# Batch 0's tail transposes, value products and squares in another order, V and w_out loads issued behind casts

## The chip, the cores and the metric

The kernel runs on one core of a Trainium2 chip. Its time is the device time of one execution in microseconds (us); lower is better. A profiled execution gives a trace of every engine: PE is TensorE (PEld its weight load), DVE is VectorE, ACT is ScalarE, POOL is GpSimd, SP is SyncE, which here only issues transfers. A "q" behind an engine's name (ACTq, SPq, POOLq) means its instruction queue, as for a DMA issue.

## The reference

Attention with a decay that depends on the position, over 8 batches of 8 heads, 576 positions and 64 numbers per head, and behind it a gated feed-forward network (FFN) over all 4608 tokens:

```python
scores = scale * np.matmul(q, k.transpose(0, 1, 3, 2))
cum = np.cumsum(np.maximum(s, 0.0), axis=-1)
bias = -(cum[:, :, :, None] - cum[:, :, None, :])
scores = np.where(causal, -1000000000.0, scores + np.minimum(bias, 0.0))
attn = softmax(scores)                       # rows, with the max taken off
x = np.matmul(attn, v)                       # then heads side by side: 4608 x 512

rms = np.sqrt(np.mean(x * x, axis=-1, keepdims=True) + 1e-06)
xn = x / rms * rms_g
g = xn @ w_gate                              # 512 x 1536
silu = g * (1.0 / (1.0 + np.exp(-g)))
val = xn @ w_val                             # 512 x 1536
out = silu * val @ w_out                     # 1536 x 512
```

All inputs and the output are float32. The kernel takes scores only between neighbouring blocks of 128 positions (the decay makes the others vanish) and checks at the end that this was allowed; a general version stands behind a branch.

## The kernel before

**Tiling.** A batch has five blocks of positions, four of 128 and a tail of 64 ("the tail" below), and its heads come in two halves, g = 0 for heads 0 to 3 and g = 1 for heads 4 to 7. The FFN goes over nine chunks of 512 tokens. A chunk has 12 gate blocks and 12 value blocks, each of four 128x512 matmuls (lines 730 and 739), and then four output blocks of 12 matmuls (line 752). Between a gate and a value block ACT takes the tanh (`T`, line 733), and DVE makes `U` from it (line 742) and `Ht` from U and the value block (lines 735 and 747).

**PSUM.** The banks are shared by tags: `psF` (four banks, for the FFN and for some transposes and scores), `psS` (two banks for one pair of scores), `psAV` (one bank, value products of g = 0) and `psT` (one bank, transposes and value products of g = 1). A new tile of a tag waits until the readers of the bank's last tile are done.

**Attention of one batch.** `load_kq` and `load_kq_tail` bring k and q as float32, `cast` and `cast_x` turn them into bfloat16 (`kqn`), `t_step` and `tail_step` transpose them on PE into `kqT` (tail_step, line 211: eight transposes for the two tails into one bank, and two copies by DVE for batch 0, lines 222 and 226). `s_step` makes scores of a key block with two query blocks and the exponentials `E` on ACT (line 299; line 315 for batch 0). `av_step` (line 333) multiplies E by V; a column of ones in `v_sb` gives the row sums, DVE takes their reciprocal (line 354) and scales (line 356) into `x_sb`. Its `norm` is a square with a running sum, on ACT (line 363) or DVE (line 367). `alpha` (two POOL operations, lines 376 and 379) makes 1/rms from it, `x_scale` (DVE, line 386) applies 1/rms and the gain, and x is transposed into `xnT`, by PE (`xt_step`, line 406) or by a DMA on SP's queue (`xt_dma`, line 397). Of batch 1, block (1,3) goes through PE, blocks 0 to 2 by DMA.

**The prologue** (lines 845 to 986) is an order written out by hand: each engine gets its instructions in the order of the text and waits where data are missing. It loads batch 0, transposes it, takes its scores (`s_first(kb, g)`: key block and half), value products (`do_av((0, qb, g))`), squares, alphas and four scalings, and transposes x for the first chunk. `fold_v` (POOL, line 330) multiplies V of batch 0 by the decay before its product. The gain is turned into a column (`g_col`, line 955) and spread over all rows in a bank (`gq`, line 958), which the first scalings read. `warm` and `stir` are matmuls without use. Behind the first scaling, SP issues four loads of k and q of batch 1.

**The FFN with attention in between.** After each gate and value block, and after each four output matmuls, `step` (line 655) advances a slot counter (36 slots a chunk) and places one piece of attention. In order it emits what is pending (the second half of a score's exponentials and its mask), a scaling that is due, one entry of `act_side` (loads on ACT's queue), then at odd slots one of `v_side` (loads on POOL's queue), then one of `pool_side`, then PE's pieces (`place`), then one of `dve_side`. Each entry has a condition, mostly a least slot. In chunk 0 `v_side` stops at slot 24, and `pool_side` from slot 30 to 33.

For chunk 0 the entries stand in lines 995 to 1016. On `pool_side` at slot 4, 6 and 8 are casts of batch 1 (`piece1`; that of slot 8 is q of heads 4 to 7), on `v_side` at slot 7 V blocks 0 and 1 of batch 1, at slot 9 w_out in two halves, then three more V blocks. `loads(2, 1, later, 14)` puts the q load of batch 2 on `act_side` from slot 14, its tail three slots later, and notes that slot as `raw`. `casts(2)` (line 495) puts five casts of that q and `over(1)`, which only notes the slot and queues later loads and transposes, on `pool_side`, each in a slot of its own, from seven slots after `raw`. In chunk 0 a slot is some 1.1 to 1.2 us.

Of the kernel before, what the change touches and what calls it, by code (L numbers as in the profile page):

```python
# [26 lines left out]
def kernel(  # L27
# [12 lines left out]
    nc = tc.nc  # L40
# [6 lines left out]
    NSC = 5  # L47
# [6 lines left out]
    def rows(c):  # L54
        return 128 if c < 4 else 64
# [49 lines left out]
    def psF():  # L105
        return pp.tile([128, DM], FP32, name="psF", tag="F", bufs=4)
# [10 lines left out]
    def psAV16():  # L117
        return pp.tile([128, 8, 128], BF16, name="psAV16", tag="AV", bufs=1)

    def psT():  # L120
        return pp.tile([128, 8, 128], BF16, name="psT", tag="T", bufs=1)

    def psT32():
        return pp.tile([128, 512], FP32, name="psT32", tag="T", bufs=1)


    def load_kq(eng, b, w, h0=0, h1=H):
        src = k if w == 0 else q
        eng.dma_start(
            out=kq32[:, w, h0:h1, 0:256],  # L130
            in_=src[b, h0:h1, 0:512, :].rearrange("h (p r) d -> p h (r d)", r=4))

    def load_kq_tail(eng, b, w):
        src = k if w == 0 else q
        eng.dma_start(
            out=kq32[0:64, w, :, 256:320],
            in_=src[b, :, 512:576, :].rearrange("h p d -> p h d"))

    def cast(eng, b, w, r0, r1, h0=0, h1=H):
        o = kqn[:, b % 2, w, r0:r1, h0:h1, :]  # L140
        i = kq32[:, w].rearrange("p h (r d) -> p r h d", d=D)[:, r0:r1, h0:h1, :]
        if eng is nc.scalar:
            eng.activation(out=o, in_=i, func=AF.Copy)
        else:
            eng.tensor_copy(out=o, in_=i)

    def cast_x(eng, b, w, hp):

        if hp < HP:
            o = kqn[:, b % 2, w, 0:4].rearrange("p r h d -> p (r h d)")[:, hp * 512:hp * 512 + 512]  # L150
            o = o.rearrange("p (r h d) -> p h r d", r=4, h=2)
            i = kq32[:, w, 2 * hp:2 * hp + 2, 0:256].rearrange("p h (r d) -> p h r d", d=D)
            eng.tensor_copy(out=o, in_=i)
        else:
            cast(eng, b, w, 4, 5)

    def load_k(b, c):
        n = rows(c)
        nc.gpsimd.dma_start(
            out=kqn[0:n, b % 2, 0, c],  # L160
            in_=k[b, :, c * 128:c * 128 + n, :].rearrange("h p d -> p h d"))
# [19 lines left out]
    def load_v(b, c):  # L181
        n = rows(c)
        nc.gpsimd.dma_start(  # L183
            out=v_sb[0:n, b % 2, c, :, 0:64],
            in_=v[b, :, c * 128:c * 128 + n, :].rearrange("h p d -> p h d"))
# [22 lines left out]
            out=kqTn[:, b % 2, w, hp:hp + 2, 0:512].rearrange("d h (p r) -> d h p r", r=4),  # L208
            in_=pT.rearrange("d (h r) p -> d h p r", r=4))

    def tail_step(b):
        pT = psT()
        nw = 2 if b < XB else 1
        for w in range(nw):
            for hp in range(HP):
                i = w * HP + hp
                nc.tensor.matmul(
                    pT[:, i, :], lhsT=kqn[:, b % 2, w, 4, 2 * hp:2 * hp + 2, :],
                    rhs=ident_bf, is_transpose=True, start=(i == 0), stop=(i == nw * HP - 1))
        dst, src = kqTn[:, b % 2, 0, :, 512:576], pT[:, 0:HP, 0:64]  # L220
        if b == 0:
            nc.vector.tensor_copy(out=dst, in_=src)
        else:
            nc.scalar.activation(out=dst, in_=src, func=AF.Copy)
        if nw == 2:
            nc.vector.tensor_copy(out=kqTn[:, b % 2, 1, :, 512:576], in_=pT[:, HP:8, 0:64])
# [147 lines left out]
    def alpha(c0, c1, n=128):  # L374

        nc.gpsimd.tensor_scalar(  # L376
            out=al_all[0:n, c0:c1], in0=ss_all[0:n, c0:c1],
            scalar1=1.0 / DM, scalar2=EPS, op0=ALU.mult, op1=ALU.add)
        nc.gpsimd.tensor_tensor(  # L379
            out=al_all[0:n, c0:c1], in0=al_all[0:n, c0:c1],  # L380
            in1=mhalf[0:n, 0:c1 - c0], op=ALU.pow)
# [50 lines left out]
    done = {}  # L432
# [10 lines left out]
    pool_side, dve_side, v_side, act_side = [], [], [], []  # L443
    x_seq = []

    def at(*key):
        return done.get(key, 10 ** 6)

    def ready(lag, *key):
        return at(*key) + lag <= slot[0]  # L450
# [31 lines left out]
    def loads(b, w, when, lag):  # L482

        def main():
            load_kq(nc.scalar, b, w)
            last["L"] = slot[0]

        def tail():
            load_kq_tail(nc.scalar, b, w)
            done["raw", b, w] = last["L"] = slot[0]  # L490
        n = len(act_side)
        when(act_side, lag, [main, tail])
        act_side[n:] = [(lambda c=c: c() and slot[0] - last["L"] >= 3, f) for c, f in act_side[n:]]

    def casts(b):

        def key(c):
            load_k(b, c)  # L500
            done["K", b, c] = slot[0]
            if c == NSC - 1:
                check(b)

        def over(w):
            done["cast", b, w] = slot[0]
            if b + 1 < B and (w == 1 or b + 1 < KB):
                loads(b + 1, w, early, 4)
            if w == 1:
                x_seq.extend((b, ww, c) for c in range(NSC) for ww in ((1, 0) if b >= KB else (1,)))  # L510
            else:
                done["cast", b] = slot[0]
                check(b)

        def free(w):
            return ready(0, "check", b - 2, w) and (
                ready(0, "T", b - 2) if w == 0 and b < KB + 2 else
                b < XB + 2 or ready(4, "X", b - 2, w, 4))
        if b >= KB:
            pool_side.extend((lambda: free(0) and slot[0] % 2 == 0, lambda c=c: key(c)) for c in range(NSC))  # L520
        fns = [(1, lambda r=r: cast_x(nc.gpsimd, b, 1, r)) for r in range(NSC)]
        fns += [(1, lambda: over(1))]
        if b < KB:
            fns += [(0, lambda r=r: cast(nc.gpsimd, b, 0, r, r + 1)) for r in range(NSC)]
            fns += [(0, lambda: over(0))]
        pool_side.extend((lambda w=w: ready(7, "raw", b, w) and free(w), f) for w, f in fns)

    def after_tail(b):
        if b + 2 < B:
# [32 lines left out]
    def do_av(key, ps=None, act=False, apart=False):  # L562
        b, qb, g = key
        act = act or b > 1 or b == 1 and qb > 1
        norm = av_step(b, qb, g, ps, act)
        if g == 1 and not apart:
            norm()
        done["AV", b, qb, g] = slot[0]
        last["AV"] = slot[0]
        if b > 0 and g == 1:  # L570
            last["AVT"] = slot[0]
        if qb == 4 and g == 1:
            if b == 0:
                nc.vector.memset(v_sb[:, 0, :, :, 64:65], 1.0)
            after_av(b)
        return norm
# [190 lines left out]
    def load_wout(f0):  # L767
        nc.gpsimd.dma_start(
            out=wout_sb[:, f0:f0 + 6, :],
            in_=moe_w_out[f0 * 128:(f0 + 6) * 128, :].rearrange("(fc p) d -> p fc d", p=128))  # L770
# [74 lines left out]
    with tc.manual_schedule():  # L845
# [37 lines left out]
        def pairF():  # L883
            return (psF(), psF())

        def s_first(kb, g, pair=None):
            do_s((0, kb, g), pair)()
# [51 lines left out]
            fold_v(POOL, c)  # L939
        load_w(moe_w_gate, wg_sb, 3, 6)  # L940
        s_first(0, 1, pairF())
        s_first(1, 1)
        tail_step(0)
        done["T", 0] = 0
        s_first(2, 1, pairF())
        do_av((0, 0, 0))
        norms = [do_av((0, 0, 1), psT32(), act=True, apart=True)]
        s_first(3, 0)
        do_av((0, 1, 0))
        s_first(3, 1, pairF())  # L950
        norms += [do_av((0, 1, 1), psT32(), act=True, apart=True)]
        ps = psS()
        gq = ps[:, 0, :]
        nc.tensor.matmul(ps[:, 1, 0:CC], lhsT=g_in, rhs=ident_f[0:CC, 0:CC], is_transpose=True)
        nc.vector.tensor_copy(out=g_col, in_=ps[:, 1, 0:CC])
        do_av((0, 2, 0))
        for c in range(CC):
            nc.tensor.matmul(gq[:, c * 128:(c + 1) * 128],
                             lhsT=g_col[:, c:c + 1].to_broadcast([128, 128]), rhs=ident_f,
                             is_transpose=True, start=(c == 0), stop=(c == CC - 1))  # L960
        norms += [do_av((0, 2, 1), psT32(), act=True, apart=True)]
        do_av((0, 3, 0))
        norms += [do_av((0, 3, 1), psT32(), act=True, apart=True)]
        for norm in norms:
            norm(False)
        alpha(0, 2)
        alpha(2, 3)
        alpha(3, 4)
        warm(4)
        for qb in range(4):  # L970
# [24 lines left out]
        def put(queue, n, *fns):  # L995
            queue.extend((lambda: slot[0] >= n, f) for f in fns)
# [7 lines left out]
        put(v_side, 1, lambda: load_w(moe_w_gate, wg_sb, 6, 12))  # L1004
        put(v_side, 3, lambda: (load_w(moe_w_val, wv_sb, 6, 9), load_w(moe_w_val, wv_sb, 9, 12)))
        put(v_side, 5, lambda: (load_tail(0), load_tail(1)))
        put(v_side, 7, lambda: (load_v(1, 0), load_v(1, 1)))
        put(v_side, 9, lambda: (load_wout(0), load_wout(6)))
        later(v_side, 0, [
            lambda: load_v(1, 2), lambda: load_v(1, 3), lambda: load_v(1, 4)])  # L1010

        loads(2, 1, later, 14)
        loads(2, 0, later, 24)
        check(0, (0,))
        check(1)
# [193 lines left out]
```

## Time and profile before

| | us |
|---|---|
| median of 3 runs (lowest, highest) | 366.95 (366.31, 367.0) |
| the profiled execution's own time | 365.93 |
| its span, first to last instruction | 364.3 |
| first FFN matmul (chunk 0) | 27.68 |
| first matmul of chunk 1 on record | 69.40 |
| last output copy on ACT ends | 359.2 |

Busy time in some stretches of the span, in us:

| stretch | length | PE | DVE | ACT | POOL |
|---|---|---|---|---|---|
| 15.61 to 20.20 | 4.59 | 4.59 | 2.21 | 4.17 | 4.57 |
| 20.20 to 22.98 | 2.78 | 1.98 | 2.07 | 2.15 | 1.80 |
| 42.00 to 58.00 | 16.00 | 15.92 | 14.63 | 13.38 | 9.77 |
| 58.00 to 66.00 | 8.00 | 8.00 | 5.56 | 5.21 | 6.29 |
| 246.00 to 282.00 | 36.00 | 36.00 | 23.88 | 26.69 | 9.43 |

Loads of the stretch around the change, from issue to landing in us: V blocks of batch 1, in order, 8.1, 8.0, 16.0, 15.9 and 13.9; the two halves of w_out 8.7 and 14.3; q of batch 2 12.5 and its tail 9.7.

How to read the lines below: start and duration in us, engine, source line, operation, tile written from tile read, shapes, count, and in brackets how long the engine was idle before and what released it. Lines with a count are several instructions in one row. A matmul's duration includes its way through the array, so consecutive ones overlap; their spacing counts.

### The profile page before, as it was taken

The page shows a single profiled execution, that of the slowest core. Times are in us where ns is not written, and L with a number is a line of the kernel's source. Part 1 is how long each engine was busy: PE and PEld are TensorE (multiplying, and loading weights), DVE is VectorE, ACT ScalarE, POOL GpSimd, SP SyncE. Part 2 cuts the span into 40 slices and gives each one's busy share as a digit, 9 for nine tenths or more (in the row PEclk, how much of TensorE's full clock was granted, in tenths as well). Part 3 has the DMA queues.
Part 4 walks back from the last instruction along what each step waited for, and adds up shares of the span by engine and source line. Part 5 has one row for each costly group of instructions (what it writes and reads, how often), then busy time and mean ns, then how long its engine had stood idle before and what let it go on. Part 6 is the DMA issues. An engine that isn't in the chain of part 4 may idle for free. (4 is left out here: it accounts for less than half of the span.)

```text
span 364.3 us, 6978 instructions
## 1 busy us (share of the span) xinstructions
PE 350.6 (96%) x2383; PEld 161.5 (44%) x2383; DVE 274.2 (75%) x523; ACT 237.1 (65%) x612; POOL 176.3 (48%) x286
## 2 busy tenths in 40 slices
PE   5889999999999999999999999999999999999993
PEld 2445444443444444444444444444444444444441
DVE  6687988599887889689989889884588558827830
ACT  3978686467885788876787777777677644223321
POOL 6958848739556466879648823732222200000000
PEclk9999999999999999999999999999999999999999
DMA  7999999999959399949979944972300130020011
GB/s 224 130 189 291 186 239 204 185 219 192 187 139 108 69 191 141 168 120 163 167 198 173 144 109 106 108 95 59 101 14 17 43 108 3 0 88 29 1 47 73
DMA packets 126592, 45.81 MB, mean 126 GB/s; under 512 B 104980, under 2 KB 121880, under 8 KB 126552
## 3 DMA queue, kind: packets, MB, share of 16 engines
q0 software_dynamic: 62048, 11.93, 45.9%
q1 hardware_dynamic: 51872, 23.80, 31.1%
q10 hardware_dynamic: 12632, 9.59, 10.9%
q8 instruction: 19, 0.31, 0.4%
q14 instruction: 21, 0.17, 0.2%
HBM read 37.90 MB, written 9.44 MB: 130 GB/s over the span
## 5 line engine op out<-in xcount | busy, mean ns | idle before, releaser
L299 ACT ACTIVATE E<-psS,biasK 128x256 bf16<-128x256 f32 (+3 forms) x328 | 106.9, 413 | 19.5 <-PE psS L275 19.1
L730 PE MATMUL psF<-xnT,wg_sb 128*128 128x512 bf16 x432 | 111.1, 379 | 0.7 <-DVE U L742 0.4
L739 PE MATMUL psF<-xnT,wv_sb 128*128 128x512 bf16 x432 | 111.1, 379 | 0.0
L752 PE MATMUL psF<-wout_sb,Ht 128*128 128x512 bf16 x432 | 102.3, 379 | 0.0
L742 DVE SCALAR_TENSOR_TENSOR U<-T,psF 128x512 bf16<-128x512 f32 x108 | 73.6, 682 | 29.5 <-ACT T L733 29.5
L733 ACT ACTIVATE T<-psF 128x512 f32<-128x512 f32 x108 | 64.4, 597 | 43.6 <-PE psF L730 40.6
L308 POOL TENSOR_SCALAR_AFFINE_SELECT E<-E 128x512 bf16<-128x512 bf16 x64 | 45.3, 708 | 86.4 <-ACT E L299 86.0
L735 DVE TENSOR_TENSOR Ht<-U,psF 128x512 bf16<-128x512 bf16 x99 | 67.6, 683 | 7.1 <-PE psF L739 0.5
L730 PEld LDWEIGHTS <-wg_sb 128*128 128x128 bf16 x432 | 38.7, 98 | 45.6 <-issue 6.4
L752 PEld LDWEIGHTS <-Ht 128*128 128x128 bf16 x432 | 38.7, 98 | 42.1 <-issue 2.3
L739 PEld LDWEIGHTS <-wv_sb 128*128 128x128 bf16 x432 | 38.5, 98 | 42.4 <-issue 4.4
L757 ACT ACTIVATE osb<-psF 128x512 f32<-128x512 f32 x36 | 21.4, 595 | 34.4 <-PE psF L752 28.6
L386 DVE SCALAR_TENSOR_TENSOR xs_sb<-x_sb,al_all,g_row 128x512 bf16<-128x512 bf16 (+1 forms) x36 | 29.3, 813 | 12.7 <-POOL al_all L379 12.7
L183 POOL DMA_DIRECT2D v_sb<-in_v_dram x40 | 34.8, 872 | 0.3 <-issue 0.3
L363 ACT ACTIVATE xs_sb<-x_sb 128x512 bf16<-128x512 bf16 (+1 forms) x37 | 23.5, 636 | 16.4 <-DVE x_sb L356 16.3
L424 DVE TENSOR_TENSOR acc<-acc,mag 128x1280 bf16<-128x1280 bf16 x32 | 27.2, 862 | 0.2
L275 PE MATMUL psS<-kqT 64*128 64x256 bf16 (+2 forms) x304 | 25.9, 256 | 0.9 <-ACT kqT L200 0.5
L347 PEld LDWEIGHTS <-E 128*128 128x128 bf16 x320 | 21.7, 97 | 10.1 <-issue 0.2
L379 POOL TENSOR_TENSOR al_all<-al_all,mhalf 128x1 f32<-128x1 f32 (+2 forms) x39 | 22.9, 586 | 3.2
L341 PEld LDWEIGHTS <-E 128*128 128x128 bf16 x256 | 20.0, 98 | 7.8 <-DVE x_sb L356 0.6
L275 PEld LDWEIGHTS <-kqT 64*128 64x128 bf16 x320 | 9.4, 94 | 30.8 <-issue 29.5
L376 POOL TENSOR_SCALAR al_all<-ss_all 128x1 f32<-128x1 f32 (+2 forms) x39 | 9.6, 247 | 23.3 <-ACT xs_sb L363 20.1
(119 smaller groups left out, 300.3 us busy)
## 6 DMA issues: line engine op xcount, KB each, us to landing
out_dram<-osb SPq DMA_DIRECT2D x36, 256.0 KB, 2.2
kq<-in_q_dram ACTq DMA_DIRECT2D x6, 1024.0 KB, 7.2
v_sb<-in_v_dram POOLq DMA_DIRECT2D x32, 128.0 KB, 6.6
kq<-in_k_dram SPq DMA_DIRECT2D x4, 512.0 KB, 5.8
kq<-in_q_dram SPq DMA_DIRECT2D x4, 512.0 KB, 7.7
kq<-in_k_dram ACTq DMA_DIRECT2D x2, 1024.0 KB, 8.9
kqn<-in_k_dram POOLq DMA_DIRECT2D x16, 128.0 KB, 5.5
wout_sb<-in_moe_w_out_dram POOLq DMA_DIRECT2D x2, 768.0 KB, 11.5
```

The source lines that it names most:

```text
L183: nc.gpsimd.dma_start(out=v_sb[0:n, b % 2, c, :, 0:64], in_=v[b, :, c * 128:c * 128 + n, :].rearrange("h p d -> p h d"))
L275: nc.tensor.matmul(pair[par][:, j * W:j * W + M], lhsT=kT, rhs=qT, start=(j == 0 and not premask), stop=(j == nj - 1))
L299: nc.scalar.activation(out=eo, in_=ei, func=AF.Exp, scale=0.125, bias=biasK[:, kb, bh:bh + 1])
L308: nc.gpsimd.affine_select(out=Ev[:, :, 0:nq], in_=Ev[:, :, 0:nq], pattern=[[0, nh], [1, nq]], compare_op=ALU.is_ge, fill=0.0, base=0, chan ...
L386: nc.vector.scalar_tensor_tensor(out=xs_sb[0:n, (b * NSC + qb) % NX, :], in0=x_sb[0:n, (b * NSC + qb) % NX, :], scalar=al_all[0:n, col:col ...
L424: nc.vector.tensor_tensor(out=acc[:, sl], in0=acc[:, sl], in1=mag[:, sl], op=ALU.max)
L730: nc.tensor.matmul(Gp, lhsT=wg_sb[:, cc, fs], rhs=xnT[:, cc, x0:x0 + DM], start=(cc == 0), stop=(cc == CC - 1))
L733: nc.scalar.activation(out=T, in_=Gp, func=AF.Tanh, scale=0.5)
L735: nc.vector.tensor_tensor(out=Ht[:, fb - 1, :], in0=pend[0], in1=pend[1], op=ALU.mult)
L739: nc.tensor.matmul(Vp, lhsT=wv_sb[:, cc, fs], rhs=xnT[:, cc, x0:x0 + DM], start=(cc == 0), stop=(cc == CC - 1))
L742: nc.vector.scalar_tensor_tensor(out=U, in0=T, scalar=1.0, in1=Gp, op0=ALU.add, op1=ALU.mult)
L752: nc.tensor.matmul(Op, lhsT=Ht[:, fb, tb * 128:(tb + 1) * 128], rhs=wout_sb[:, fb, :], start=(fb == 0), stop=(fb == FB - 1))
```

## The change

In the prologue, the tail transposes of batch 0 go into the bank of `psAV` instead of `psT`, and stand before the scores of key block 1 for heads 4 to 7. The value products of block 1 both stand before the last scores, (3, 1). The squares (`norms`), which stood together behind all value products, are put one by one: the first ahead of the exponentials of (3, 1), the second behind them, the third and fourth each behind its own value products. The alphas are grouped 0, then 1 and 2, then 3, instead of 0 and 1, then 2, then 3. The g transposes stand between the two halves of block 3.

In chunk 0, V of batch 1 goes from slot 7 to 9, w_out from 9 to 11, so the three V blocks behind move by two slots too; q of batch 2 goes from slot 14 to 17. The five q casts of batch 2 begin five instead of seven slots after `raw`, and the last one and `over(1)` share a slot.

```diff
-    def tail_step(b):
-        pT = psT()
+    def tail_step(b, pT=None):
+        pT = psT() if pT is None else pT
@@
         fns = [(1, lambda r=r: cast_x(nc.gpsimd, b, 1, r)) for r in range(NSC)]
-        fns += [(1, lambda: over(1))]
+        if b == 2:
+            fns[-1] = (1, lambda: (cast_x(nc.gpsimd, b, 1, NSC - 1), over(1)))
+        else:
+            fns += [(1, lambda: over(1))]
...
-        pool_side.extend((lambda w=w: ready(7, "raw", b, w) and free(w), f) for w, f in fns)
+        pool_side.extend((lambda w=w: ready(5 if (b, w) == (2, 1) else 7, "raw", b, w) and free(w), f) for w, f in fns)
@@
         s_first(0, 1, pairF())
+        tail_step(0, psAV16())
+        done["T", 0] = 0
         s_first(1, 1)
-        tail_step(0)
-        done["T", 0] = 0
         s_first(2, 1, pairF())
         do_av((0, 0, 0))
         norms = [do_av((0, 0, 1), psT32(), act=True, apart=True)]
         s_first(3, 0)
         do_av((0, 1, 0))
+        norms += [do_av((0, 1, 1), psT32(), act=True, apart=True)]
+        norms[0](False)
+        alpha(0, 1)
         s_first(3, 1, pairF())
-        norms += [do_av((0, 1, 1), psT32(), act=True, apart=True)]
+        norms[1](False)
         ps = psS()
         gq = ps[:, 0, :]
         nc.tensor.matmul(ps[:, 1, 0:CC], lhsT=g_in, rhs=ident_f[0:CC, 0:CC], is_transpose=True)
+        do_av((0, 2, 0))
         nc.vector.tensor_copy(out=g_col, in_=ps[:, 1, 0:CC])
-        do_av((0, 2, 0))
+        norms += [do_av((0, 2, 1), psT32(), act=True, apart=True)]
+        norms[2](False)
+        alpha(1, 3)
+        do_av((0, 3, 0))
         for c in range(CC):
             nc.tensor.matmul(gq[:, c * 128:(c + 1) * 128],
                              lhsT=g_col[:, c:c + 1].to_broadcast([128, 128]), rhs=ident_f,
                              is_transpose=True, start=(c == 0), stop=(c == CC - 1))
-        norms += [do_av((0, 2, 1), psT32(), act=True, apart=True)]
-        do_av((0, 3, 0))
         norms += [do_av((0, 3, 1), psT32(), act=True, apart=True)]
-        for norm in norms:
-            norm(False)
-        alpha(0, 2)
-        alpha(2, 3)
+        norms[3](False)
         alpha(3, 4)
@@
-        put(v_side, 7, lambda: (load_v(1, 0), load_v(1, 1)))
-        put(v_side, 9, lambda: (load_wout(0), load_wout(6)))
+        put(v_side, 9, lambda: (load_v(1, 0), load_v(1, 1)))
+        put(v_side, 11, lambda: (load_wout(0), load_wout(6)))
...
-        loads(2, 1, later, 14)
+        loads(2, 1, later, 17)
```

## The prediction

> **What bounds the kernel.** I read the page's first part, then the busy time by stretch, then the timeline of the two places that the diff touches.
>
> ```profile
> PE 350.6 (96%) x2383; PEld 161.5 (44%) x2383; DVE 274.2 (75%) x523; ACT 237.1 (65%) x612; POOL 176.3 (48%) x286
> ```
>
> ```profile
> 22.98:27.68 4.70, 3.92 (x34) 1.75 (x31) 4.63 (x13) 3.61 (x9) 1.65 (x5) 1.00 1.15 229
> 27.68:42.00 14.32, 13.98 (x108) 7.25 (x108) 11.53 (x23) 10.05 (x23) 13.38 (x23) 1.00 1.32 249
> 174.00:210.00 36.00, 36.00 (x259) 16.20 (x258) 32.45 (x59) 27.87 (x79) 24.83 (x39) 1.00 1.55 168
> ```
>
> After the stretch and its length come busy time and count of PE, PEld, DVE, ACT and POOL, then the granted clock, the DMA share and GB/s. From 27.68, where the first chunk of the FFN begins, PE is full, at clock 1.00. So what moves the end is time without useful PE work: the prologue up to 27.68, and stalls later. A late step costs later chunks nothing more. Four 128x512 matmuls take 0.865 from start to start, four transposes 0.22; beyond such spacings, chunk 0 loses 0.87 at 38.65, 0.14 at 33.63 and 0.14 at 50.55.
>
> **The prologue** ends in a chain over ACT, DVE and POOL:
>
> ```profile
> 17.12 0.29 DVE L222 COPY kqT<-psT 128x256 bf16<-128x256 bf16 x1 [2.29 <-PE psT L217]
> 17.87 1.09 ACT L315 ACTIVATE E<-psF 128x512 bf16<-128x512 f32 x2 [0.21 <-PE psF L275]
> ...
> 22.71 0.63 ACT L363 ACTIVATE xs_sb<-x_sb 128x512 bf16<-128x512 bf16 x1 [0.63 <-DVE x_sb L356]
> 22.73 0.20 PE L341 MATMUL psT<-v_sb,E 128*128 128x65 bf16 x1 [0.49 <-DVE x_sb L356]
> ...
> 23.40 0.42 DVE L356 TENSOR_TENSOR x_sb<-psT,rZ 128x256 bf16<-128x256 f32 x1
> ...
> 23.74 0.74 DVE L386 SCALAR_TENSOR_TENSOR xs_sb<-x_sb,al_all,psS 128x512 bf16<-128x512 bf16 x1
> ```
>
> Two things are visible. The tail transposes stand on PE between the scores of key blocks 1 and 2, and ACT is idle 0.21 for it. The value products hand psAV and psT back and forth with DVE, and the last half, at 22.73, waits for DVE; behind it come the four scalings, the transposes and the first FFN matmul.
>
> Tail step: 8 transposes cost 0.46 (16.46 to 16.92). Moved behind scores (0,1), they run at 15.23 to 15.69, while PE waits for psS until 15.61 anyway: 0.08 lost there. psAV was free since the copy of the paired transposes at 13.37. The two tail copies (0.29 and 0.28) fall into DVE's 2.29 of idling; that cover gone, they would cost 0.5. Exponentials (1,1) then start at 16.65, (2,1) at 17.73 instead of 17.87, (3,0) at 18.81 instead of 18.95.
>
> Value products: from PE start to the reciprocal 0.45 (18.84 to 19.29), then 0.22 to the scaling, 0.42 for it, 0.06 to hand the bank back. Block 0 starts at 17.39, its halves are scaled by 18.92; block 1 runs at 18.58 and 18.97, now ahead of scores (3,1), which go to 19.22. The v_sb fold of block 1 ends on POOL at 18.50: hidden by 0.08. Block 2 starts at 20.17 and 20.42; its second scaling, now behind the g_col copy (0.15), ends at 21.88. Block 3 starts at 21.32; the four g transposes (0.48) stand between its halves, so the second starts at 22.05 and its scaling at 22.72, 0.68 before 23.40. Squares take 0.61 on ACT: the first at 19.6, hence exponentials (3,1) at 20.26 instead of 19.99, which nothing needs before 22.05. The third starts at 21.92 instead of 22.71; 1.81 later (as 21.36 to 23.17 shows for a pair of columns) its alpha is ready, 23.73, and the second scaling goes at 23.78 instead of 24.47. The POOL operations of alpha stay six, grouped otherwise. I take **-0.65**; bounds -0.1 (one more handover of 0.55 comes in) and -0.8 (the third square's gain). SP's four loads for batch 1 come 0.65 earlier too, behind the scaling.
>
> **The stall at 38.65:**
>
> ```profile
> 35.86 1.79 POOL L183 DMA_DIRECT2D v_sb<-in_v_dram  x2
> 37.64 1.98 POOL L145 CAST kqn<-kq 128x256 bf16<-128x256 f32 x4
> ...
> 38.98 0.10 PEld L192 LDWEIGHTS <-kqn 128*128 128x128 bf16 x1 [0.25 <-POOL kqn L145]
> 39.51 0.68 DVE L367 SCALAR_TENSOR_TENSOR xs_sb<-x_sb 64x512 bf16<-64x512 bf16 x1
> ...
> 40.18 0.73 DVE L198 COPY kqT<-psT 128x512 bf16<-128x512 bf16 x1
> 40.83 0.66 DVE L735 TENSOR_TENSOR Ht<-U,psF 128x512 bf16<-128x512 bf16 x1
> 42.12 1.03 PE L730 MATMUL psF<-xnT,wg_sb 128*128 128x512 bf16 x4
> ```
>
> PE's transposes wait for POOL's casts, which stand behind two V issues (1.79). With V at slot 9 the casts run 35.9 to 37.4, done 1.2 before 38.65; their data (q, heads 4-7) landed at 35.05. PE gains up to 0.87, but DVE does not: from 38.26 it works back to back, and its copy at 40.18 starts as the square ends. The bank of the seventh gate block (42.12) is freed by Ht at 40.83 + 0.66 + 0.06 = 41.55. PE, 0.87 earlier, would start it at 41.25; it gets 41.5. The eighth is met (wanted at 43.68, its U done at 42.80 + 0.68 + 0.06 = 43.54), the ninth about met (46.25 against 46.32). So 0.6 of 0.87 stays: **-0.6**, bounds 0 (DVE's later steps take the rest) and -1.0 (DVE catches up in its 0.81 idle at 49.0, and the two waits of 0.14 go).
>
> What is moved behind: V(1,0), V(1,1), then w_out, then three V loads, in the same order on POOL's queue. Landings were 43.96 and 44.75, needed at 46.72; w_out 48.3 and 54.7, needed at 56.63 and about 58.3; V(1,2) landed at 58.1, needed at 58.73. That queue works without a break, so landings follow the queue, not the issue. The q load of batch 2 (1024 KB) on ACT's queue starts three slots later and leaves it room. Cost 0, up to +0.6 if V(1,2) lands when it did, as PE asks 1.2 earlier.
>
> **The cast merged with `over`.** `raw` is three slots later and the lag two less, so the five q casts of batch 2 shift by one slot; `over` stays at slot 29. The first is now behind alpha(1,1), the last between alpha(1,2) and alpha(1,3):
>
> ```profile
> 60.44 0.60 POOL L153 CAST kqn<-kq 128x512 bf16<-128x512 f32 x1
> 60.51 1.08 DVE L386 SCALAR_TENSOR_TENSOR xs_sb<-x_sb,al_all,g_row 128x512 bf16<-128x512 bf16 x1 [0.41 <-POOL al_all L379]
> 64.69 0.75 DVE L386 SCALAR_TENSOR_TENSOR xs_sb<-x_sb,al_all,g_row 128x512 bf16<-128x512 bf16 x1 [0.69 <-POOL al_all L379]
> 64.84 0.65 POOL L376 TENSOR_SCALAR al_all<-ss_all 128x1 f32<-128x1 f32 x1 [0.18 <-ACT xs_sb L363]
> 66.97 0.40 PE L406 MATMUL psT<-ident_bf,xs_sb 128*128 128x128 bf16 x4
> ```
>
> A cast just ahead of a scaling makes it 1.08 instead of 0.75. The last cast would start at 64.65, so: scaling (1,2) to 65.77, alpha(1,3) 0.48 later than now, and the transposes at 66.97, ready with no slack, 0.49 late. Chunk 1 starts at 69.40 only because xnT of block (1,2) lands at 69.27, 0.23 behind PE. So 0.49 - 0.23 = **+0.26**; bounds 0 (alpha's 0.65 at 64.84 shows it already blocked until the scaling ended) and +0.5.
>
> The Trainium skill, "SBUF — State Buffer", section "Who interferes with whom", says of this pair that VectorE operations with two SBUF inputs and a GpSimd operation that reads SBUF hold a shared port in turn, and the later one blocks entirely. By it the scaling would wait for the whole cast (0.6, where the row shows 0.33 of lengthening), and the item would be +0.5 and the sum -0.75.
>
> **Sum:** -0.65 - 0.6 + 0.26 = -1.0. Against the profiled execution (365.93, its span 364.3 and 1.6 around it) that is 364.9; the shown runs have a median 1.0 higher, 366.95, so **365.95**.
>
> **Cases.** About 0.2%, 0.73, is what a measurement can tell from no change.
> - Likeliest, **0.46**: as summed. Its own range is 365.5 to 366.5.
> - More, **0.20**: DVE catches up (-1.0), the cast is free: -1.65, 365.3. For it: DVE's idle 0.81 at 49.0. Against: the bank at 41.55.
> - Handed over, **0.24**: DVE's chain or V(1,2) takes back the whole of the second gain, leaving -0.65 + 0.26: 366.55. This is also what remains if the change does its new order but the stall merely moves. For it: DVE is busy 14.63 of 16.00 from 42 to 58; against: the banks' room.
> - Slower, **0.10**: the q load lands late.
>
> ```profile
> 43.60 0.40 ACTq L129 DMA_DIRECT2D kq<-in_q_dram  x1
> 47.97 0.65 ACTq L135 DMA_DIRECT2D kq<-in_q_dram  x1
> ```
>
> It took 12.5 to land at 56.10. Issued at slot 17 (now 47.97, less 1.2) it lands at 59.25, and POOL wants it at 60.44 - 1.2 = 59.24. On POOL the masks, alpha(1,2) and alpha(1,3) stand behind the waiting cast, and chunk 1's start behind those: each us late is a us. It is slower than before from 13.5 of landing on; at 14.25, half way to the slowest load of that stretch (16.0), it is 1.75 late: 367.7. Against it: POOL's queue, relieved until then, will have less left.
>
> Faster: 0.38 + 0.20 + 0.02 = 0.60. Same: 0.08 + 0.22 + 0.02 = 0.32. Slower 0.08. The range 365.1 to 367.1 leaves out about 0.07 below and 0.09 above.
>
> **What would show it.** Right: tail copies at about 16 on DVE; the first FFN matmul at 27.0; transposes after the second value step of block 4 at normal 0.22; a PE wait on Ht of some 0.25 before the seventh gate block; casts of batch 2 with no wait on DMA; the transposes of block (1,3) some 0.5 late by their spacing. Wrong: the first matmul at 27.5 or later, a PE wait for V in chunk 0's output part, POOL idle for kq.

## The result and the profile after

| | before | after |
|---|---|---|
| median of 22 runs each (lowest, highest), us | 367.0 (365.81, 367.87) | 368.76 (366.3, 371.57) |
| profiled execution, its span, us | 365.93, 364.3 | 368.94, 367.4 |
| first FFN matmul, us | 27.68 | 26.90 |
| first matmul of chunk 1 on record, us | 69.40 | 72.42 |
| from there to the end of the span, us | 294.9 | 295.0 |

The changed kernel is slower: ratio 1.0048, 95% interval 1.0027 to 1.0069, some 1.8 us. The last row places the loss: behind chunk 1's start the two profiled executions are alike, and chunk 0, from its first FFN matmul to chunk 1's, takes 45.5 us instead of 41.7. In the changed kernel the lines behind the prologue are numbered three higher (line 730 is 733, 752 is 755).

The page's first part and PE's useful work are as before:

```profile
PE 351.7 (96%) x2383; PEld 161.7 (44%) x2383; DVE 273.9 (75%) x523; ACT 237.1 (65%) x612; POOL 176.8 (48%) x286
```

The prologue went as intended. These lines are from the timeline of after (start, duration, engine, line, operation):

```profile
15.73 0.29 DVE L222 COPY kqT<-psAV 128x256 bf16<-128x256 bf16 x1 [0.64 <-PE psAV L217]
...
22.62 0.42 DVE L356 TENSOR_TENSOR x_sb<-psT,rZ 128x256 bf16<-128x256 f32 x1
22.96 0.74 DVE L386 SCALAR_TENSOR_TENSOR xs_sb<-x_sb,al_all,psS 128x512 bf16<-128x512 bf16 x1
...
26.90 1.02 PE L733 MATMUL psF<-xnT,wg_sb 128*128 128x512 bf16 x4 [0.25 <-ACT xnT L413]
```

The tail copies stand at 15.73 instead of 17.12, the last scaling of a value product at 22.62 instead of 23.40, the first FFN matmul 0.78 earlier.

Then chunk 0 loses it, and more. ACT's, POOL's and PE's timelines of after, up to and behind the stall that the change was to remove:

```profile
30.11 1.34 ACT L143 ACTIVATE kqn<-kq 128x256 bf16<-128x256 f32 x4 [1.55 <-DMA kq<-in_k_dram]
...
38.78 1.57 POOL L145 CAST kqn<-kq 128x256 bf16<-128x256 f32 x4 [2.13 <-DMA kq<-in_q_dram]
39.38 1.26 PE L192 MATMUL psT<-ident_bf,kqn 128*128 128x128 bf16 x4
40.30 1.79 POOL L183 DMA_DIRECT2D v_sb<-in_v_dram  x2
...
42.96 1.73 POOL L771 DMA_DIRECT2D wout_sb<-in_moe_w_out_dram  x2
...
45.27 0.90 POOL L183 DMA_DIRECT2D v_sb<-in_v_dram  x1
```

The kernel before issues V ahead of these casts, as the prediction showed, and w_out right behind them:

```profile
39.57 1.64 POOL L768 DMA_DIRECT2D wout_sb<-in_moe_w_out_dram  x2
...
42.08 0.95 POOL L183 DMA_DIRECT2D v_sb<-in_v_dram  x1
```

q of heads 4 to 7 of batch 1, issued at 25.47 instead of 26.25, landed at 38.8 instead of 35.0. POOL idles 2.13 for it. Its casts end at 40.35 instead of 39.62, by then as far behind before as PE is, so PE's four transposes are stretched from 0.4 to 1.26 as before. V now stands behind the waiting casts, with w_out behind it: they are issued 4.4 and 3.4 later than before, V of block (1,2) 3.2 later.

The DMA view of before, from 40 to 46 us, shows the busy share of the DMA engines in 40 slices, then queue, packets, MB moved and the time of the packets:

```profile
DMA  9999999999999999999999999999999999999999
q0 software_dynamic: 3809, 1.06, 204.3%
```

The same view of after:

```profile
DMA  9999645455533597999999966999999977199411
q0 software_dynamic: 2918, 0.47, 115.2%
```

q0 carries what POOL issues. It moves 0.47 MB instead of 1.06, and the DMA engines are about half idle from 40.6 to 42.1 and nearly idle from 45.5 on: little is queued. The end of chunk 0 pays for it (PE's timeline of before, then of after):

```profile
58.77 0.20 PE L347 MATMUL psAV<-v_sb,E 128*128 128x65 bf16 x1
...
69.40 1.02 PE L730 MATMUL psF<-xnT,wg_sb 128*128 128x512 bf16 x4
```

```profile
60.28 0.19 PE L347 MATMUL psAV<-v_sb,E 128*128 128x65 bf16 x1 [0.77 <-DMA v_sb<-in_v_dram]
72.39 0.56 PEld L733 LDWEIGHTS <-wg_sb 128*128 128x128 bf16 x4 [1.71 <-DMA xnT<-xs_sb]
72.42 1.02 PE L733 MATMUL psF<-xnT,wg_sb 128*128 128x512 bf16 x4 [1.61 <-DVE mag L418]
```

V of block (1,2) lands at 60.3 instead of 58.1, and PE waits 0.77 for it. xnT of block (1,2) lands at 72.3, and chunk 1 starts after a wait of 1.61, where the row of before names none (0.23 by the spacing). The last two lines are the same wait; the row of PE names `mag` of DVE, which has nothing to do with the FFN, the row of PEld names the DMA that was late.

The losses of chunk 0 against before, by the spacings of PE: transposes at 30.68 +0.67 and at 33.61 +0.74, at 39.38 0 (0.87 in both), V +0.92, chunk 1's start +1.54, and 0.14 less, which before lost at 50.55. That is 3.73 of the 3.80. The first two follow the row of ACT above: k of heads 0 to 3, issued 0.77 earlier, landed at 30.1 instead of 28.8, and ACT waits 1.55 for it. Beyond the usual spacing PE loses 1.55 at these two places in after and 0.13 in before, but also 1.10 to 1.57 in e3, e7 and e12 below, which have the prologue of before: it is the spread of k's landing in the main.

### The profile page after: what moved, and what is told of

Read it like the earlier page. It is cut to its first block, busy times and chain, and to the rows that moved or that the text cites. A ratio compares the mean times of both kernels' runs of the same rounds, so it can differ in the third digit from the quotient of the medians.

```text
span 367.4 us, 6978 instructions
## 1 busy us (share of the span) xinstructions
PE 351.7 (96%) x2383; PEld 161.7 (44%) x2383; DVE 273.9 (75%) x523; ACT 237.1 (65%) x612; POOL 176.8 (48%) x286
## 5 line engine op out<-in xcount | busy, mean ns | idle before, releaser
L755 PEld LDWEIGHTS <-Ht 128*128 128x128 bf16 x432 | 38.7, 98 | 42.1 <-issue 2.3
L760 ACT ACTIVATE osb<-psF 128x512 f32<-128x512 f32 x36 | 21.4, 595 | 35.6 <-PE psF L755 29.7
L275 PEld LDWEIGHTS <-kqT 64*128 64x128 bf16 x320 | 9.3, 94 | 30.7 <-issue 29.5
## 6 DMA issues: line engine op xcount, KB each, us to landing
wout_sb<-in_moe_w_out_dram POOLq DMA_DIRECT2D x2, 768.0 KB, 10.2
```

The costliest lines, as they stand in the source:

```text
L275: nc.tensor.matmul(pair[par][:, j * W:j * W + M], lhsT=kT, rhs=qT, start=(j == 0 and not premask), stop=(j == nj - 1))
L755: nc.tensor.matmul(Op, lhsT=Ht[:, fb, tb * 128:(tb + 1) * 128], rhs=wout_sb[:, fb, :], start=(fb == 0), stop=(fb == FB - 1))
```

## The experiments

P is the prologue's order alone, V the two slot numbers of V and w_out, Q the later q load of batch 2 with its casts; the change is P, V and Q together. Each row of the table has the median, the ratio to before, run beside it on the same chip, with its 95% interval, and from the profiled execution: the landing of batch 1's q of heads 4 to 7, the landing of V of block (1,2), PE's wait for that V, and PE's wait at chunk 1's start. Waits are those in the brackets of PE's rows, 0 where there is none. A landing is the issue plus a duration given to a tenth, so it is good to 0.1.

| kernel | us | ratio | q | V(1,2) | V wait | chunk 1 wait |
|---|---|---|---|---|---|---|
| before | 367.0 | | 35.0 | 58.1 | 0 | 0 |
| after (P, V, Q) | 368.76 | 1.0048 (1.0027 to 1.0069) | 38.8 | 60.3 | 0.77 | 1.61 |
| e1: P | 366.71 | 0.998 (0.9961 to 0.9999) | 34.6 | 59.1 | 0.62 | 0.47 |
| e2: V | 370.41 | 1.009 (1.0067 to 1.0113) | 33.8 | 60.6 | 2.13 | 0 |
| e3: Q | 367.65 | 1.0004 (0.9984 to 1.0024) | 38.4 | 59.5 | 0 | 1.40 |
| e4: V, Q | 367.74 | 1.0016 (0.9993 to 1.0039) | 35.7 | 59.3 | 0.89 | 1.32 |
| e5: P, V | 367.34 | 1.0021 (0.9996 to 1.0046) | 36.4 | 60.6 | 1.74 | 0.81 |
| e6: P, Q | 366.82 | 0.9994 (0.997 to 1.0017) | 37.6 | 58.2 | 0 | 1.19 |
| e7: V, w_out in slot 9 | 368.23 | 1.0025 (0.9999 to 1.0051) | 38.9 | 61.5 | 1.74 | 0.67 |
| e8: P, V(1,2) earlier | 366.43 | 0.9981 (0.9968 to 0.9995) | 35.7 | 53.1 | 0 | 0.41 |
| e9: P, V, Q, V(1,2) earlier | 366.69 | 1.0009 (0.9984 to 1.0033) | 35.2 | 49.1 | 0 | 1.20 |
| e10: P, V(1,1) later | 366.73 | 0.998 (0.9959 to 1.0) | 40.0 | 54.4 | 0 | 0.41 |
| e12: before, q late | 366.99 | 1.0008 (0.9987 to 1.0029) | 38.3 | 59.9 | 0.17 | 0.15 |
| e13: P, V, Q, q late | 368.13 | 1.003 (1.0011 to 1.005) | 36.6 | 59.8 | 1.66 | 1.48 |
| e14: P, Q, q late | 367.02 | 0.9992 (0.9974 to 1.0009) | 38.0 | 59.1 | 0 | 1.83 |

One profile is one execution, and executions of one kernel spread over 2 to 5 us here; the profile shows by which way time is lost, the ratio how much on the whole. Most kernels ran ten or more times, e2 only four times. The landing of q moves between 33.8 and 40.0 with no order by P, V or Q.

Of the expectations below, those of e1, e6, e7 and e9 were met by the ratio, in the range of the theory named first. e2 lost far more than expected, e3, e4, e5, e12, e13 and e14 less; e8 and e10 gained less, and e11 went the other way.

### The three parts alone: e1, e2, e3

e1 takes the prologue of the change alone:

```diff
+        tail_step(0, psAV16())
         s_first(1, 1)
-        tail_step(0)
...
+        norms += [do_av((0, 1, 1), psT32(), act=True, apart=True)]
+        norms[0](False)
         s_first(3, 1, pairF())
-        norms += [do_av((0, 1, 1), psT32(), act=True, apart=True)]
```

> Only the prologue's new order; loads and casts at the slots of before. Theory 'late loads': the first FFN matmul moves from 27.7 to about 26.9 as in the changed kernel, but the batch 1 loads of k and q do not land earlier, so the casts wait for them and give back part: 0 to -0.8 us against before. No wait of chunk 1 for xnT beyond 0.3. Rival 'earlier loads collide': the four loads, issued 0.77 earlier into the weight loads, land several us later, stalls of 0.7 to 0.9 at the transposes of batch 1, and most of the loss of the whole change is here: +1 to +2 us.

e2 takes the slots of V and w_out alone:

```diff
-        put(v_side, 7, lambda: (load_v(1, 0), load_v(1, 1)))
-        put(v_side, 9, lambda: (load_wout(0), load_wout(6)))
+        put(v_side, 9, lambda: (load_v(1, 0), load_v(1, 1)))
+        put(v_side, 11, lambda: (load_wout(0), load_wout(6)))
```

> Only V of batch 1 at slot 9 and w_out at 11. Theory 'late loads': the casts of slot 8 run right behind those of slot 6 if q has landed (35.05 in before), so the stall of 0.87 goes, DVE takes some back, and V block 2 lands later than PE wants it: -0.6 to +0.4 us. Rival: nothing lands later, -0.6 us.

e3 takes q of batch 2 at slot 17 with its shifted and merged casts alone:

```diff
-        loads(2, 1, later, 14)
+        loads(2, 1, later, 17)
...
+        if b == 2:
+            fns[-1] = (1, lambda: (cast_x(nc.gpsimd, b, 1, NSC - 1), over(1)))
```

> Only q of batch 2 at slot 17 with its casts one slot later, the last merged with over. Theory 'late loads': the traffic of ACT's queue moves into the time of the xnT transposes by DMA, of which the last then takes 6 us instead of 3.8; chunk 1 starts 1.0 to 1.5 us later by its own wait: +1.0 to +1.5 us. Rival: 0 to +0.3 us (the merged cast alone).

P alone is 0.7 us faster (0.998), its first FFN matmul at 27.08. V alone is slower by 0.9%, more than the whole change. Its PE timeline shows both sides of the edit:

```profile
38.41 0.39 PE L192 MATMUL psT<-ident_bf,kqn 128*128 128x128 bf16 x4
...
41.36 1.02 PE L730 MATMUL psF<-xnT,wg_sb 128*128 128x512 bf16 x4 [0.19 <-DVE Ht L735]
...
60.71 0.21 PE L347 MATMUL psAV<-v_sb,E 128*128 128x65 bf16 x1 [2.13 <-DMA v_sb<-in_v_dram]
```

Where q lands in time (33.8), the stall of 0.87 is gone, the transposes take 0.39, and a short wait on Ht stands in its place. The price comes 19 us later: 2.13 of waiting for V. Here the DMA engines are full from 40 to 46 in nearly every slice, but q0 moved 0.87 MB, not 1.06; the thin part is 43 to 45, with 0.27 MB where before has 0.39.

Q alone shows no difference in the ratio, against the +1.0 to +1.5 expected. Its profile has no wait for V, and a wait of 1.40 at chunk 1: the last transpose of x by DMA took 5.2 instead of 3.8.

### The parts in pairs: e4, e5, e6

e4 joins the edits of e2 and e3, e5 those of e1 and e2, e6 those of e1 and e3:

```diff
 # e4, e5
-        put(v_side, 7, lambda: (load_v(1, 0), load_v(1, 1)))
+        put(v_side, 9, lambda: (load_v(1, 0), load_v(1, 1)))
 # e4, e6
-        loads(2, 1, later, 14)
+        loads(2, 1, later, 17)
 # e5, e6
+        tail_step(0, psAV16())
```

> All of the chunk 0 schedule (V, w_out, q, casts), prologue as before. Theory 'late loads': V block 2 awaited 0.5 to 0.8 us, chunk 1 late by 1.4: +1 to +2 us, about the loss of the whole change plus the prologue's gain of 0.8. Rival 'earlier loads collide': -0.6 to +0.2 us.

> Prologue and V, w_out behind the casts, q of batch 2 at slot 14 as before. Theory 'queue runs dry': V and w_out, issued behind casts that wait for q of batch 1, leave POOL's transfer queue short of work between 40 and 46 us, V block 2 lands 2 us or more later, and q of batch 2 ahead of it makes it worse: +2 to +3 us against before. Rival 'sum of parts' (prologue -0.7, V and w_out +3.0): +2.3. What tells them apart is in the trace: bytes of that queue from 40 to 46 below 0.9 MB (before 1.06) and the landing of V block 2 at 60 or later.

> The whole change without V and w_out behind the casts. Theory 'queue runs dry': the loss of the whole change (+1.8) goes: -0.9 to +0.3 us against before, 1.5 or more below the whole change. Rival 'the late q costs chunk 1': still +0.7 or more, by a wait for xnT at the start of chunk 1.

Adding V raises the ratio in all four pairs: by 0.90% to before, 0.41% to P, 0.12% to Q, 0.54% to P and Q; on the mean 0.49%, 1.8 us. Adding Q gives +0.04, +0.14, -0.74 (to V) and +0.27%, about nothing. Adding P gives -0.20, -0.69, -0.10 and +0.32%, on the mean -0.17%. Single differences carry an uncertainty of some 0.3%, and the large ones, 0.90, -0.74 and -0.69, all rest on the four executions of e2, so only the signs of V and the means are used; without the pair of e2, V's mean is 0.36%, 1.3 us. A PE wait for V(1,2) of 0.77 to 2.13 is in all four kernels with V, and in those without it is 0.62 once and 0 else; a wait of 1.2 to 1.6 at chunk 1 is in all four with Q, and 0 to 0.81 in those without.

### Why V(1,2) is late: e7, e8, e9, e10

e7 moves V behind the casts and leaves w_out in its slot, so only V's 1.8 us of issue go past the casts:

```diff
-        put(v_side, 7, lambda: (load_v(1, 0), load_v(1, 1)))
-        put(v_side, 9, lambda: (load_wout(0), load_wout(6)))
+        put(v_side, 9, lambda: (load_v(1, 0), load_v(1, 1), load_wout(0), load_wout(6)))
```

> Before with V blocks 0 and 1 in slot 9, together with w_out, which so keeps its slot; the last three V blocks go from 11, 13, 15 to the same slots. Only the order V behind casts differs. Theory 'queue runs dry': V lands about as before, w_out later by the 0.9 that the two V issues take behind the casts less the stall they leave, V block 2 some 0.5 to 1.5 later than before: +0.3 to +1.5 us, well under the 3.0 of the full two-slot shift. Rival 'V behind casts alone is the loss': +3 us.

e8 has the prologue of the change, V(1,0) and V(1,1) as before, and V(1,2) between the halves of w_out (in e8, e9 and e10 it leaves the list of V loads behind them):

```diff
-        put(v_side, 9, lambda: (load_wout(0), load_wout(6)))
+        put(v_side, 9, lambda: (load_wout(0), load_v(1, 2)))
+        put(v_side, 11, lambda: load_wout(6))
```

> The prologue's new order, and V block 2 of batch 1 issued between the two halves of w_out; all else as before. Theory: in every run PE waits for V block 2 at the first value product of the output part, or only just does not; landed by 55 it takes 0.6 to 0.8 out of the prologue version, unless the second half of w_out or V block 3 then comes late: -0.8 to -1.6 us against before. Rival: the bound is the sum of the traffic and another transfer is late in its place (V block 3, xnT): -0.3 to -0.8, as the prologue alone.

e9 does this in the whole change, with the halves at slots 11 and 13:

```diff
-        put(v_side, 11, lambda: (load_wout(0), load_wout(6)))
+        put(v_side, 11, lambda: (load_wout(0), load_v(1, 2)))
+        put(v_side, 13, lambda: load_wout(6))
```

> The whole change, but V block 2 of batch 1 is issued between the halves of w_out (slots 11 and 13). Theory 'queue runs dry': the wait for V block 2 (0.8 in the whole change's profile) goes, the wait for xnT at the start of chunk 1 (1.2 to 1.6 in all kernels with the late q) stays: +0.3 to +1.2 us against before, some 0.8 under the whole change. Rival: the second half of w_out is late in its place: as the whole change, +1.8.

e10 keeps V(1,0) ahead of the casts and puts V(1,1) behind them, with V(1,2) ahead of the second half of w_out:

```diff
-        put(v_side, 7, lambda: (load_v(1, 0), load_v(1, 1)))
-        put(v_side, 9, lambda: (load_wout(0), load_wout(6)))
+        put(v_side, 7, lambda: load_v(1, 0))
+        put(v_side, 9, lambda: (load_v(1, 1), load_wout(0), load_v(1, 2)))
+        put(v_side, 11, lambda: load_wout(6))
```

> The prologue, V block 0 alone ahead of the casts of slot 8, V block 1 and V block 2 around the first half of w_out at slot 9, the second half at 11. Theory: the casts start 0.9 earlier, so the stall at the transposes of heads 4 to 7 shrinks from 0.87 to 0.2 or less where q has landed in time, and only one issue is held up where it hasn't: -0.8 to -1.6 us against before. Rival: w_out behind two V issues runs late: -0.3 to +0.5.

In e7 q landed at 38.9, though its prologue is that of before; POOL waited 2.23, V was issued at 40.37, q0 moved 0.64 MB from 40 to 46, and V(1,2) came at 61.5. In e8 and e9 V(1,2) comes at 53.1 and 49.1 and PE waits for no V. e8's POOL and PE timelines:

```profile
40.36 0.89 POOL L183 DMA_DIRECT2D v_sb<-in_v_dram  x1
...
69.76 1.02 PE L730 MATMUL psF<-xnT,wg_sb 128*128 128x512 bf16 x4 [0.41 <-DVE rZ L354]
```

So the V wait can be taken away by the order within POOL's queue, and with it the loss is no longer seen: e9 stands at 1.0009 where the whole change was 1.0048. e9's median is below before's, but four of its twelve executions took over 368, so its ratio is not below 1. e8, at 0.9981, is level with P alone (0.998): the wait of 0.62 in P's profile is gone, and the ratio shows no gain from it. e10 gives what P gives too: a split of the two V blocks brings nothing more. In its profiled execution, the slowest of its twelve (368.63), q came at 40.0, the stall grew to some 1.7, and q0 moved only 0.49 MB from 40 to 46; yet PE waited for no V, since V(1,2) stood ahead of the second half of w_out.

Bytes of q0 by stretch, in MB, tell how a late start reaches V(1,2):

| | 40 to 46 | 46 to 54 | V(1,2) lands |
|---|---|---|---|
| before | 1.06 | 1.00 | 58.1 |
| e2 | 0.87 | 1.01 | 60.6 |
| e4 | 0.87 | 1.20 | 59.3 |
| after | 0.47 | 1.40 | 60.3 |

In e4 and after, where q of batch 2 on ACT's queue (q10) comes later, part of what is lost by 46 is made up (issued at 47.41 and 48.73; 42.84 in e2, which makes up nothing). And once V's own turn has come, it shares with that load. The DMA view of after from 56 to 58:

```profile
q10 hardware_dynamic: 491, 0.48, 88.0%
q0 software_dynamic: 490, 0.06, 47.3%
```

Packet for packet the two get the same, byte for byte V gets an eighth, since its packets are small. The Trainium skill, "DMA: Bandwidth & Descriptors", section "Queues, rings and completion order", says that a DMA engine goes round the queues that have work and changes at packet boundaries. The equal counts of these two rows agree, and so do 238 against 240 packets in before from 50 to 52.

### The start of chunk 1: e11

P and Q with the load of k of batch 2 six slots later, to keep it away from the transposes of x by DMA:

```diff
-        loads(2, 0, later, 24)
+        loads(2, 0, later, 30)
```

> Prologue and late q of batch 2, with k of batch 2 six slots later too (30 instead of 24). Theory: chunk 1 waits for the last xnT transfer because q's and k's traffic on ACT's queue runs beside it; with k later, that wait falls from 1.2 to 0.4 or less: 0.6 to 1.0 us under the same kernel with k at 24 (which was level with before). Rival: the wait comes from the scaling and its alpha behind the shifted casts on POOL, and stays at 1.2: no change.

It took 386.69, ratio 1.0516 (1.0493 to 1.054): PE has new waits from 80 us on, the longest 2.88; that k, issued at 62.35, came too late for batch 2 is the likely reason and was not traced. Chunk 1's wait stayed at 1.39, and k still ran beside the last transfer, from 62.4 to 69.2. The run does not separate the theories. What it shows on the side: the first transpose of x by DMA, ahead of k's load, took 5.5, where the other profiles have 8.2 to 9.5 with k beside it.

The queues during the last transfer show the same. Before, from 66 to 68 (q1 is SP's queue):

```profile
q1 hardware_dynamic: 791, 0.41, 116.2%
```

After, same stretch:

```profile
q1 hardware_dynamic: 341, 0.31, 52.4%
q0 software_dynamic: 480, 0.06, 46.5%
q10 hardware_dynamic: 480, 0.18, 39.9%
```

Before, SP's queue has the engines nearly for itself; in after, the tail of k of batch 2 (issued on ACT's queue at 61.56 instead of 60.05, landed in 10.2 instead of 5.7) and POOL's loads share them, and the transfer takes 6.1 instead of 3.8.

### A q of batch 1 made late: e12, e13, e14

The load of q of heads 4 to 7 goes behind the four scalings, some 2 us later, in before (e12), in the whole change (e13) and in P with Q (e14):

```diff
-                for g in (0, 1):
-                    for w in (0, 1):
-                        load_kq(nc.sync, 1, w, 4 * g, 4 * g + 4)
+                for g, w in ((0, 0), (0, 1), (1, 0)):
+                    load_kq(nc.sync, 1, w, 4 * g, 4 * g + 4)
...
+        load_kq(nc.sync, 1, 1, 4, 8)
```

> Before, with one load moved: q of batch 1, heads 4 to 7, is issued on SP's queue behind the first check of magnitudes, some 2 us later, so that it always lands late. V and w_out stand ahead of the casts that wait for it. Theory 'a late q holds V and w_out only where they stand behind the casts': the stall at the transposes of heads 4 to 7 grows by what the landing is later than 37.6, w_out is held too, as it is behind the casts also here, but V isn't: +1 to +2 us against before. Rival: a late q costs both orders the same.

> The whole change with the same load moved. Theory: V, w_out and all behind are held by the casts, POOL's queue carries under 0.6 MB from 40 to 46 us, V block 2 lands at 60.5 or later: +3 to +4.5 us against before, 1.5 or more over the kernel of before with the same load moved. Rival: as far above it as the whole change is above before (1.8), or less.

> The whole change without V and w_out behind the casts, with the same load moved. Theory: as before with the load moved, less the prologue's 0.7, plus the wait for xnT: +0.8 to +2 us against before, 1.5 or more under the whole change with the load moved. Rival: level with the whole change with the load moved.

In the order of before a q that lands at 38.3 costs nothing that the ratio shows (up to 1.1 us by its interval): V stands ahead of the waiting casts and w_out right behind them, they were issued at 36.69 and 40.41, and q0 moved 0.96 MB from 40 to 46. e14 says the same with P and Q. In the whole change the load landed at 36.6, earlier than in the profile of after itself, so e13 did not make the case worse than it was; it lies at 1.003, 1.1 us, where +3 to +4.5 was expected. The theory that a late q alone makes the loss falls by e2 (q at 33.8, V wait 2.13). It does add: in after the late q took the gain of the second part away and held V and w_out for 2.13 more.

## Why the prediction was wrong

Forecast were 365.95 and a range up to 367.1; the median is 368.76.

**The prologue, -0.65: right up to the first FFN matmul, and not all of it is kept.** That matmul came 0.78 earlier in the two profiles, and e1's ratio is worth 0.7 us (0.0 to 1.4 by its interval). Over all profiles it stands at 27.2 to 27.7 with the old prologue and at 26.4 to 27.3 with the new, 0.5 earlier on the mean. That SP's four loads "come 0.65 earlier too" was right for their issue (0.77), but not for their landing: k came at 29.7 on the mean with the old prologue and at 29.5 with the new. So ACT, which casts this k, waits longer, and behind the transposes that follow (33.99 in before) PE is ahead by 0.2 on the mean, not 0.5 (six executions with the old prologue, ten with the new). That k and q landed later in after than in before does not need the earlier issue: e3 and e7, with the old prologue, had q at 38.4 and 38.9, and e1, with the new, at 34.6.

**The stall at 38.65, -0.6 of 0.87: right where q lands in time, and not so in the profile of after.** e2, e4 and e5 lost the stall and showed the wait on Ht that was foretold (0.25; measured 0.18 to 0.19 as a wait, 0.35 by the spacing in e2). But the step took q as landed at 35.05, the value of one execution, in which there were 2.6 us to the casts at 37.64. Moving V behind the casts spends that cover, and the landing spreads over 6 us. In after POOL waited, and PE's stall was 0.87 as before.

**V and w_out behind the casts, cost 0: this is the step that failed.** It read: "That queue works without a break, so landings follow the queue, not the issue." POOL's transfer queue was full in before because V was issued ahead of the casts and w_out right behind them. Issued later, they leave a gap: 0.47 to 0.90 MB instead of 1.06 from 40 to 46 in every kernel with V, and in after DMA engines that are half idle for a time. The gap is passed on to V(1,2), which had 0.63 to spare (58.1 against 58.73) and comes 1.2 to 2.5 later in the four kernels with V. Its "up to +0.6 if V(1,2) lands when it did" was no upper bound: that bound took the landing as fixed and let only PE move. Measured over four pairs, V costs about 1.8 us, its gain at the stall included, where -0.6 was forecast.

**The q load three slots later, "leaves it room": right, and not free.** It relieves V(1,2), whose wait falls from 2.13 to 0.89 between e2 and e4, and vanishes from e1 to e6. With it, more of batch 2's loads lies beside the last transpose of x for chunk 1, and PE waits 1.2 to 1.8 there in every kernel with Q; that the one makes the other is argued from the queues' rows, since e11 did not separate it. The two about cancel: Q's mean effect is nil.

**The merged cast, +0.26: the start of chunk 1 is late, but by another way.** POOL, DVE and PE in the timeline of after:

```profile
61.18 0.62 POOL L308 TENSOR_SCALAR_AFFINE_SELECT E<-E 128x512 bf16<-128x512 bf16 x1
61.25 1.10 DVE L386 SCALAR_TENSOR_TENSOR xs_sb<-x_sb,al_all,g_row 128x512 bf16<-128x512 bf16 x1
...
64.93 0.60 POOL L145 CAST kqn<-kq 128x512 bf16<-128x512 f32 x1
65.43 0.74 DVE L386 SCALAR_TENSOR_TENSOR xs_sb<-x_sb,al_all,g_row 128x512 bf16<-128x512 bf16 x1
66.36 0.19 POOL L376 TENSOR_SCALAR al_all<-ss_all 128x1 f32<-128x1 f32 x1 [0.83 <-ACT xs_sb L363]
67.22 0.75 DVE L386 SCALAR_TENSOR_TENSOR xs_sb<-x_sb,al_all,g_row 128x512 bf16<-128x512 bf16 x1 [1.04 <-POOL al_all L379]
68.45 0.39 PE L406 MATMUL psT<-ident_bf,xs_sb 128*128 128x128 bf16 x4
```

The cast ends 0.10 after the scaling begins, and the scaling takes 0.74, as one that is alone. The transposes at 68.45 follow without the 0.5 of delay that was named as a sign. Where a scaling started beside a POOL instruction that had longer to run, it was held: at 61.25, beside a mask to 61.80, it took 1.10 and ended 0.55 after the mask; in before the one at 60.51 ended 0.55 after the cast beside it (61.04), and six more in before 0.54 to 0.55 after theirs. Alone a scaling takes 0.75, so by estimate 0.2 of it passes while it is held and the rest comes after the POOL instruction's end. At 65.43 the 0.10 that was left of the cast fell within that 0.2, so it cost nothing. The Trainium skill, "SBUF — State Buffer", section "Who interferes with whom", says that the later one of such a pair blocks entirely. These ends agree with it; the prediction's reckoning by that rule, a lengthening by the whole cast, left out the 0.2. The wait at chunk 1 came from xnT by DMA, whose landing the step had taken as 69.27 unmoved.

**The rivals.** "Handed over" named V(1,2) as what takes back the second gain, and that is what happened; it was capped at that gain (366.55), while the queue can lose more than PE gained. "Slower" foresaw that casts wait for a late q with POOL's work behind them, but for q of batch 2, whose casts, from 60.61 on, had no DMA wait. It was q of batch 1, and what stood behind it were the loads that the change itself had put there. Of the signs of being wrong, the PE wait for V in the output part and POOL's idle time for kq both came true; the first matmul was early, as forecast.

**What stays open.** What sets the landing of batch 1's loads is not settled. In after, all but a few packets of q had passed by 36 (16 more by 38); the DMA view from 38 to 40 has

```profile
q0 software_dynamic: 812, 0.38, 144.6%
...
q1 hardware_dynamic: 4, 0.00, 0.6%
```

four last packets of SP's queue beside 812 of POOL's. Why these come last in some executions was not tried. How much of after's 1.8 us is the late q and how much the moved V and w_out is bounded only: e13 with q at 36.6 lost 1.1, the whole change in its own runs 1.8.

## What to carry to other kernels

Before a load is moved behind work that itself waits for a transfer, ask what the queue will carry in the meantime: a landing follows the queue only while the queue is full, and a gap is passed on to the last load in it, here some 15 us later. A landing time from one profile has a spread; a step that uses up its slack needs that spread, not the one value. When a prologue or a stall is shortened, look for the load with the least slack behind it and issue that one earlier, as e9 did with V(1,2).

## What the runs showed of the hardware

- A load issued on ACT's queue moved its first bytes late: q of batch 2, issued at 43.60 in before and 42.84 in e2, moved nothing before 46 in either, 2.4 and 3.2 later, while q0 was busy.
- Two queues that were both busy passed equal counts of packets (491 and 490 in after, 240 and 238 in before), so the load with small packets got an eighth of the bytes in the stretch of after.
- The same 512 KB load of q landed between 33.8 and 40.0 over the profiled executions, with issues that differed by 2 us or less.
- A DMA transpose of x took 3.8 in before, with hardly another queue at work, and 6.1 in after beside two others.
- A scaling on DVE that started while a POOL instruction was running ended 0.54 to 0.55 after that instruction's end (60.51 in before, 61.25 in after), where alone it takes 0.75 from start to end.
